# Attention scores on two halves of the contraction rows, with a running maximum from PSUM

## The chip, the cores and the metric

The kernel runs on one core of a Trainium2 chip. The metric is the device time in microseconds; three runs of the kernel before gave 732.77, 735.24 and 737.40 us. The times of single instructions come from one profiled execution.

## The reference, cut to what matters

```python
def _attn_ref(q, k, v):                       # 2 batches, 8 heads, 1152 rows, 64 columns, float32
    q_pool = q.reshape(B, H, S // 2, 2, D).mean(axis=3)
    scores = (1.0 / np.sqrt(D)) * np.matmul(q_pool, k.transpose(0, 1, 3, 2))
    scores = scores - np.max(scores, axis=-1, keepdims=True)
    attn = np.exp(scores)
    attn = attn / (np.sum(attn, axis=-1, keepdims=True) + 1e-09)
    return np.matmul(attn, v)
...
x = attention output as 1152 tokens x 512
x = softplus(x @ w_in1) @ w_out1              # 512 -> 2048 -> 512
h = x @ w_in2                                 # 512 -> 2048
g = (a0 + a1*h + a2*h*h + a3*h*h*h) / (1 + |b0|*|h| + |b1|*h*h + 1e-6)
out = g @ w_out2                              # 2048 -> 512
```

The queries are averaged in pairs, so a head has 576 queries and 1152 keys. The weights of the two MLPs come as 64-bit floats.

## The kernel before

Every product is wanted at nearly float32 accuracy. The kernel gets it by splitting an operand into a high half (rounded to the matmul's fast format, float32r) and a low half (the rest) and by multiplying hi x hi, hi x lo and lo x hi.

**Attention** goes through 16 heads, each in two units of 288 queries. A head loads q and k (lines 362 and 365), adds pairs of queries (line 373) and makes high and low halves in SBUF: `qs` holds hi, lo and once more the whole, `ks` holds hi and lo side by side. Line 285 is the subtraction that gives a low half, lines 270, 272 and 274 are copies on ACT, DVE and POOL; for all heads but the first this splitting is POOL's. PE transposes three blocks at a time (`trans_k`, line 395; `trans_q`, line 407), and ACT or DVE copies the result to SBUF. So a transposed key block fills all 128 contraction rows, 64 with its high half and 64 with its low half, and one block of scores takes two matmuls over 128 rows (line 487).

A unit computes scores for nine key blocks, two at a time into a tile `sc` of two PSUM banks, of which there are two in turn. ACT copies each to `st` in SBUF (line 497). When all nine are there, DVE takes the maximum over the nine blocks in one reduction (line 443); PE transposes it (450), DVE reduces it over partitions (454), PE spreads it back to all partitions (460), DVE subtracts it in two pieces of 1152 and 1440 columns (506), ACT takes the exponential (512). The first four blocks are multiplied with v in float32, the other five as high and low halves (543).

**The MLPs** go through 2 layers x 2 halves of the hidden width x 3 chunks of 384 tokens, and in each through 8 blocks of 128 hidden columns: twelve matmuls for h (663), an activation on ACT, POOL and DVE (687 to 702, or 715 to 731), and nine or twelve matmuls into four accumulating banks (745). Each weight piece is converted by three DVE instructions (621, 624, 627) and then split into halves, the high one by ACT, the low one by POOL, or by DVE for the hidden blocks in `VLO`.

**What sets the order.** Nothing is issued as it is written: each step is recorded with an engine, a duration, what it reads and writes, and a due time, and `Plan.order` places all of them by list scheduling with the durations of `act_t`, `dve_t`, `pool_t`, `pe_t`. The due times come from the tables `OFF` and `OFF2`. Each engine then works strictly in the order found. Buffers are slots in two SBUF arenas and the eight PSUM banks; `lay` sets them side by side, and a slot of the MLPs on bytes of attention is free only after attention's last tile there.

## Time and profile before

| | |
|---|---|
| median of 3 runs | 735.24 us (732.77 to 737.40) |
| span of the profiled execution | 731.1 us |
| PE, weight loads, DVE, ACT, POOL busy | 91%, 83%, 90%, 77%, 78% |
| instructions | 11574 |
| the reduction of line 443 | 32 times, 155.7 us |
| scores, line 487 | 576 matmuls of 128 rows x 288 columns |

A busy share counts the time in which an engine has at least one instruction in flight. Instructions of one engine overlap a little at their ends, so the distance between two starts is less than the duration printed. In a timeline a row is one instruction or a run of the same kind (x8), with the start of the first and the time to the end of the last. `a<-b` reads "into a from b"; `arena` and `arena_r` are the two SBUF arenas, `banks` is PSUM.

### The profile page before, as it was taken

How to read it: one execution, taken by the hardware profiler on the slowest of the kernel's cores; microseconds unless marked ns; L12 is line 12 of the kernel's file. 1: busy time of each engine (PE TensorE's matmuls, PEld its weight loads, DVE VectorE, ACT ScalarE, POOL GpSimd, SP SyncE). 2: the span in 40 equal slices, each digit the busy share in tenths (PEclk: the TensorE clock that was granted, in tenths of full speed). 3: DMA queues.
4: the chain of work that ended last, by engine and by line, in shares of the span. 5: the costliest groups of instructions: out<-in, count | busy, mean ns of one | idle time of the engine just before them, and what ended most of it. 6: DMA issues, size and time to landing. Idle time of an engine off the chain costs nothing.

```text
span 731.1 us, 11574 instructions
## 1 busy us (share of the span) xinstructions
PE 667.6 (91%) x4036; PEld 607.8 (83%) x4036; DVE 658.7 (90%) x694; ACT 566.5 (77%) x1029; POOL 567.9 (78%) x549
## 2 busy tenths in 40 slices
PE   7877888888888888869999999999999999999997
PEld 6766777777777777748999999999999899998996
DVE  4899999999999999999898898988697888879896
ACT  5777778887777777678788887878978888987764
POOL 5557686868677765669878898788999989998764
PEclk9899999999999999999999999999999999999999
DMA  8222212222121121425377678777012011211001
GB/s 210 65 59 58 58 48 52 50 57 51 48 52 51 23 83 25 139 69 160 115 234 227 203 230 260 242 256 252 30 55 61 15 30 43 59 30 44 0 31 57
DMA packets 66665, 70.02 MB, mean 96 GB/s; under 512 B 24496, under 2 KB 50096, under 8 KB 66608
## 3 DMA queue, kind: packets, MB, share of 16 engines
q1 hardware_dynamic: 66608, 69.30, 32.7%
q8 instruction: 31, 0.51, 0.3%
q14 instruction: 26, 0.21, 0.1%
HBM read 58.46 MB, written 10.78 MB: 95 GB/s over the span
## 4 chain that ended last, share of the span: by engine, by line
PE 58%; DVE 29%; issue 6%; ACT 3%; POOL 2%; DMA 1%; SPq 1%; DVEq 0%; POOLq 0%; ACTq 0%
PE banks L745 25%; PE banks L663 25%; DVE arena L443 17%; DVE arena L506 6%; PE banks L543 4%; PE banks L487 3%; DVE arena_r L272 2%; PE banks L407 1%; DVE arena L454 1%; PE banks L450 1%; POOL arena_r L285 1%; ACT arena L713 1%; DVE banks L727 1%; DMA arena<-rr 1%; DMA par<-in_moe_b_dram 1%
## 5 line engine op out<-in xcount | busy, mean ns | idle before, releaser
L285 POOL TENSOR_TENSOR arena_r<-arena,arena_r 128x512 fp32r<-128x512 f32 (+4 forms) x134 | 227.6, 1708 | 37.9 <-ACT arena_r L270 35.6
L745 PE MATMUL banks<-arena_r 128*128 128x384 f32 (+1 forms) x1008 | 212.6, 360 | 0.3 <-POOL arena_r L285 0.2
L663 PE MATMUL banks<-xh,arena_r 128*128 128x384 f32 x768 | 210.1, 337 | 2.6 <-DVE arena_r L285 1.8
L745 PEld LDWEIGHTS banks<-arena_r 128*128 128x128 f32 x1008 | 182.0, 188 | 15.8 <-POOL arena_r L285 0.6
L443 DVE TENSOR_REDUCE arena<-arena 128x288 f32<-128x2592 f32 x32 | 155.7, 4867 | 4.2 <-ACT arena L270 4.2
L270 ACT COPY arena<-banks 128x576 f32<-128x576 f32 (+4 forms) x213 | 115.3, 562 | 45.3 <-PE banks L543 26.4
L663 PEld LDWEIGHTS banks<-xh,arena_r 128*128 128x128 f32 x768 | 139.6, 188 | 6.0 <-DVE arena_r L285 3.2
L663 PE MATMUL banks<-xl,arena_r 128*128 128x384 f32 x384 | 128.8, 335 | 0.0
L727 DVE RECIPROCAL banks<-arena 128x384 f32<-128x384 f32 x48 | 122.6, 2555 | 6.5 <-ACT arena L713 5.0
L285 POOL TENSOR_TENSOR arena<-arena 128x384 f32<-128x384 f32 x96 | 98.8, 1030 | 26.2 <-ACT arena L697 19.5
L487 PE MATMUL banks<-arena_r 128*128 128x288 f32 x576 | 110.1, 315 | 0.2 <-ACT arena L270 0.2
L270 ACT CAST arena_r<-banks 128x384 fp32r<-128x384 f32 (+2 forms) x168 | 79.0, 472 | 39.2 <-PE banks L407 21.0
L506 DVE TENSOR_TENSOR arena<-arena,banks 128x1152 f32<-128x1152 f32 x64 | 93.4, 1501 | 0.6 <-PE banks L460 0.6
L487 PEld LDWEIGHTS banks<-arena_r 128*128 128x128 f32 x576 | 86.1, 191 | 6.5 <-ACT arena L270 1.6
L543 PE MATMUL banks<-arena_r 128*65 128x288 f32 (+1 forms) x480 | 87.8, 304 | 0.8 <-ACT arena_r L270 0.8
L512 ACT ACTIVATE arena<-arena 128x1152 f32<-128x1152 f32 x64 | 82.7, 1295 | 5.8 <-DVE arena L506 5.8
L270 ACT CAST arena_r<-arena 128x512 fp32r<-128x512 f32 (+2 forms) x90 | 79.9, 905 | 5.4 <-DVE arena L373 2.8
L543 PE MATMUL banks<-arena 128*65 128x288 f32 x256 | 80.0, 421 | 3.8 <-ACT arena L512 2.8
L285 DVE TENSOR_TENSOR arena_r<-banks,arena_r 128x384 fp32r<-128x384 f32 (+1 forms) x104 | 58.1, 560 | 27.6 <-ACT arena_r L270 27.2
L663 PEld LDWEIGHTS banks<-xl,arena_r 128*128 128x128 f32 x384 | 72.1, 188 | 1.1
L274 POOL TENSOR_SCALAR arena_r<-arena 96x384 fp32r<-96x384 f32 (+2 forms) x62 | 32.9, 539 | 46.2 <-PE banks L395 21.8
L719 POOL TENSOR_TENSOR arena<-arena 128x384 f32<-128x384 f32 x48 | 48.9, 1019 | 18.5 <-ACT arena L713 16.8
(54 smaller groups left out, 949.8 us busy)
## 6 DMA issues: line engine op xcount, KB each, us to landing
arena<-in_moe_w_in_dram SPq DMA_DIRECT2D x32, 512.0 KB, 4.4
arena<-in_moe_w_out_dram SPq DMA_DIRECT2D x32, 512.0 KB, 3.9
sp<-arena SPq DMA_DIRECT2D x32, 256.0 KB, 2.9
arena<-sp SPq DMA_DIRECT2D x32, 256.0 KB, 2.7
arena<-in_q_dram SPq DMA_DIRECT2D x16, 288.0 KB, 4.5
arena<-in_k_dram SPq DMA_DIRECT2D x16, 288.0 KB, 4.1
arena<-in_v_dram SPq DMA_DIRECT2D x16, 288.0 KB, 4.0
arena<-rr SPq DMA_DIRECT2D x16, 144.0 KB, 4.0
```

Source lines behind the costliest of these rows:

```text
L270: nc.scalar.copy(o, i)
L274: nc.gpsimd.tensor_scalar(out=o, in0=i, scalar1=1.0, scalar2=0.0, op0=ALU.mult, op1=ALU.add)
L285: e.tensor_tensor(out=o, in0=a, in1=b, op=ALU.subtract)
L443: P.op("V", dve_t(KC * HW), lambda: nc.vector.tensor_reduce(out=mx(), in_=st().rearrange("p c q -> p q c"), axis=AX.X, op=ALU.max), r=[(st ...
L487: nc.tensor.matmul(out=ps()[:, c, 0:HW], lhsT=kT()[:, c0 + c, :], rhs=qT[i]()[:, hf * HW:(hf + 1) * HW], start=(i == 0), stop=(i == 1),)
L506: nc.vector.tensor_tensor(out=s, in0=s, in1=mB()[:, None, :].to_broadcast([128, n, HW]), op=ALU.subtract)
L512: nc.scalar.activation(out=s, in_=s, func=AF.Exp, scale=escale)
L543: nc.tensor.matmul(out=o, lhsT=w, rhs=x, start=first, stop=last, skip_group_check=True)
L663: nc.tensor.matmul(out=hp(), lhsT=w()[:, kk * 128:(kk + 1) * 128], rhs=x[:, kk, :], start=(kk == 0 and n == 0), stop=(kk == KD - 1 and n = ...
L719: P.op("G", pool_t(CW), lambda: nc.gpsimd.tensor_tensor(out=Q(), in0=t(), in1=ah(), op=ALU.add), r=[t, ah], w=[Q], at=a("2q"))
L727: P.op("V", (69 + 6.25 * CW) / 1e3, lambda: nc.vector.reciprocal(out=h(), in_=Q()), r=[Q], w=[h], at=a("2r"))
L745: nc.tensor.matmul(out=o()[:, 0:w_], lhsT=lt, rhs=rh, start=(f == 0 and n == 0), stop=(f == FG - 1 and n == 2),)
```

## The change

Four things are changed, and the order of the whole program is found anew.

1. Queries and keys are no longer split in SBUF. PE transposes them in float32, two key blocks in one transpose (so the keys of block 2j lie on rows 0 to 63 and those of block 2j+1 on rows 64 to 127), and each pair of queries stands twice, on both halves of the rows. Out of PSUM, ACT writes the high half and DVE subtracts the low half. There are now four tensors `k1`, `k2`, `q1`, `q2`.
2. The scores of two key blocks come from six matmuls of 64 rows, three on each half of the rows, in turn, each half into its own bank; the lone ninth block takes three.
3. The maximum is kept as it goes: the scores of blocks 2 and 3 are compared with those of blocks 0 and 1 in SBUF, and those of each later pair with the running maximum `mp`, always read from the score tile in PSUM; the last block joins the two halves.
4. `VLO` is empty: POOL subtracts the low halves of all weights. The constants of the second MLP are loaded after the fifth head's reciprocals.

```diff
-VLO = (3, 4, 5, 6)
+VLO = ()
-M0 = 464.257
-WAIT = 0.2
-SLACK = 0.05
+M0 = 295.089
+QKT = 0.46
+WAIT = 0.093
+SLACK = 0.005
 def pe_t(n, cols):
-    return n * max(cols / 2.4 + 3, 107.0) / 1e3
+    return n * (cols / 2.4 + 13.5) / 1e3
...
-    r1 = lay(0, arena_r, 0, LR, ("qs", 1, 4608), ("ks", 1, 4608), *kq, *kq)
+    r1 = lay(0, arena_r, 0, LR, *kq, *kq)
...
+            def pool_q():
+                x = [qr()[:, :, r, :][:, :, None, :].to_broadcast([96, NQQ, 2, D]) for r in range(2)]
+                (nc.vector if first else nc.gpsimd).tensor_tensor(out=qm(), in0=x[0], in1=x[1], op=ALU.add)
...
+            def halves(t, n, np_, src, dst, keys, at):
+
+                hi, lo = dst
+                P.op("A", act_t(n), lambda: cp("A", hi(), src()), r=[t], w=[keys[0]], at=at)
+                P.op("V", dve_t(n), lambda: sub("V", lo(), src(), hi()), r=[t, keys[0]], w=[keys[1]], at=at)
...
+                js = [(0, 1, 2), (3, 4)][g]
...
+                for lo, hi, np_ in ((js[0], js[-1] + 1, 128),) if g == 0 else ((3, 4, 128), (4, 5, 64)):
...
-            mx = P.buf("mx", [128, HW], F32)
-            P.op("V", dve_t(KC * HW), lambda: nc.vector.tensor_reduce(
-                out=mx(), in_=st().rearrange("p c q -> p q c"), axis=AX.X, op=ALU.max),
-                r=[(st, c) for c in range(KC)], w=[mx], at=t0 + OFF['mx'] * T)
...
-                for c in range(n):
-                    for i in range(2):
+                for x, (a, y) in enumerate(((0, 0), (0, 1), (1, 0))):
+                    for i in range(n):
                         nc.tensor.matmul(
-                            out=ps()[:, c, 0:HW],
-                            lhsT=kT()[:, c0 + c, :],
-                            rhs=qT[i]()[:, hf * HW:(hf + 1) * HW],
-                            start=(i == 0),
-                            stop=(i == 1),
+                            out=ps()[:, i, 0:HW],
+                            lhsT=kT[a]()[64 * i:64 * i + 64, j, :],
+                            rhs=qT[y]()[64 * i:64 * i + 64, hf * HW:(hf + 1) * HW],
+                            start=(x == 0),
+                            stop=(x == 2),
                         )
...
+            def top(o, x, y, m, r, w):
+                P.op("V", dve_t(m * HW), lambda: nc.vector.tensor_tensor(out=o(), in0=x(), in1=y(), op=ALU.max),
+                     r=r, w=w, at=t0 + (OFF['mx'] + 0.15 * j) * T)
+
+            if j == 1:
+                top(mp, lambda: ps()[:, :, 0:HW], lambda: st()[:, 0:2, :], 2, [ps, (st, 0), (st, 1)], [mp])
+            elif n == 2 and j:
+                top(mp, lambda: ps()[:, :, 0:HW], mp, 2, [ps], [mp])
+            elif n == 1:
+                half = lambda: ps()[:, 1, 0:HW]
+                top(half, lambda: ps()[:, 0, 0:HW], lambda: mp()[:, 0, :], 1, [ps, mp], [(ps, 1)])
+                top(mx, half, lambda: mp()[:, 1, :], 1, [(ps, 1), mp], [mx])
...
-        ), w=["par"], at=M0, xfer=0.11)
+        ), r=[("rr", 4)], w=["par"], at=M0, xfer=0.11)
```

All entries of `OFF` and `OFF2` are replaced too, and the order that comes of it is best seen in the program's own rows. First DVE in the middle of attention, before, from one partition reduction of the maximum on to the next: the maximum over all keys (L443), the two subtractions (L506), the normalisation (L559, L560), an eviction of transposed keys (L272).

```order
L454 TENSOR_REDUCE arena<-banks 96x3
L443 TENSOR_REDUCE arena<-arena 128x288
L506 TENSOR_TENSOR arena<-arena,banks 128x1152
L506 TENSOR_TENSOR arena<-arena,banks 128x1440
L559 TENSOR_SCALAR arena<-arena 64x9
L560 RECIPROCAL arena<-arena 64x9
L272 COPY arena_r<-banks 128x384
```

The same place now, where L496 is the partition reduction, L543 the running maximum, L332 the low halves of a head's keys, L561 the subtraction.

```order
L496 TENSOR_REDUCE arena<-banks 96x3
L543 TENSOR_TENSOR arena<-banks,arena 128x576
L332 TENSOR_TENSOR arena_r<-banks,arena_r 128x384
L543 TENSOR_TENSOR arena<-banks,arena 128x576
L561 TENSOR_TENSOR arena<-arena,banks 128x1152
L543 TENSOR_TENSOR arena<-banks,arena 128x576
L332 TENSOR_TENSOR arena_r<-banks,arena_r 128x128
L543 TENSOR_TENSOR banks<-banks,arena 128x288
L332 TENSOR_TENSOR arena_r<-banks,arena_r 64x128
L543 TENSOR_TENSOR arena<-banks,arena 128x288
L561 TENSOR_TENSOR arena<-arena,banks 128x1440
```

The one long maximum has become five short ones, and other work stands between any two of them that hang on each other.

PE in the middle of attention, before: scores (L487) between pieces of PV (L543) and the transposes of queries (L407) and of the maximum (L450).

```order
L450 MATMUL banks<-ident,arena 96x128 x3
L543 MATMUL banks<-arena_r 65x288 x2
L407 MATMUL banks<-identr,arena_r 128x96 x3
L543 MATMUL banks<-arena_r 65x288 x2
L487 MATMUL banks<-arena_r 128x288 x8
L407 MATMUL banks<-identr,arena_r 128x96 x3
```

And now, with L529 the scores, L441 the transposes of keys, L492 and L502 those of the maximum, L598 PV:

```order
L441 MATMUL banks<-ident,arena 128x128 x3
L492 MATMUL banks<-ident,arena 96x128 x3
L598 MATMUL banks<-arena_r 65x288 x2
L529 MATMUL banks<-arena_r 128x288 x12
L598 MATMUL banks<-arena 65x288 x3
L502 MATMUL banks<-ident,arena 128x96 x3
L598 MATMUL banks<-arena 65x288
L529 MATMUL banks<-arena_r 128x288 x6
```

Scores now come in groups of six (the size printed is that of the output), and the transposes read float32 data (`ident,arena`) straight.

POOL where attention ends, before, from its last low half of probabilities (128x1440) on; L694 and the 128x384 subtractions belong to the MLP's activation, 128x512 is the low half of a weight.

```order
L285 TENSOR_TENSOR arena_r<-arena,arena_r 128x1440
L694 TENSOR_SCALAR arena<-arena 128x384
L285 TENSOR_TENSOR arena<-arena 128x384
L285 TENSOR_TENSOR arena_r<-arena,arena_r 128x512
L285 TENSOR_TENSOR arena<-arena 128x384
```

And now:

```order
L332 TENSOR_TENSOR arena_r<-arena,arena_r 128x1440
L332 TENSOR_TENSOR arena_r<-arena,arena_r 128x512
L749 TENSOR_SCALAR arena<-arena 128x384
L332 TENSOR_TENSOR arena<-arena 128x384
L332 TENSOR_TENSOR arena_r<-arena,arena_r 128x512
L332 TENSOR_TENSOR arena<-arena 128x384
L332 TENSOR_TENSOR arena_r<-arena,arena_r 128x512
```

A low half of a weight now stands beside nearly every step of the activation, where before it stood beside every second or third.

## Rows read from the trace of the kernel before

**Rows 1.** The page's first part: busy us, share of the span, instructions.

```profile
PE 667.6 (91%) x4036; PEld 607.8 (83%) x4036; DVE 658.7 (90%) x694; ACT 566.5 (77%) x1029; POOL 567.9 (78%) x549
```

**Rows 2.** Stretches: from:to, length, busy us by engine, granted clock, DMA, GB/s.

```profile
132.30:151.10 18.80, 15.84 (x117) 13.73 (x116) 18.52 (x16) 14.77 (x23) 15.42 (x15) 1.00 0.24 57
...
540.00:560.00 20.00, 20.00 (x101) 17.96 (x100) 17.85 (x17) 18.27 (x38) 19.51 (x19) 1.00 0.14 41
```

**Rows 3.** DVE's timeline over one head: start us, us, instruction.

```profile
169.85 4.87 DVE L443 TENSOR_REDUCE arena<-arena 128x288 f32<-128x2592 f32 x1
174.65 2.90 DVE L506 TENSOR_TENSOR arena<-arena,banks 128x1152 f32<-128x1152 f32 x2
177.47 0.15 DVE L559 TENSOR_SCALAR arena<-arena 64x9 f32<-64x9 f32 x1
...
177.84 0.56 DVE L272 CAST arena_r<-banks 128x384 fp32r<-128x384 f32 x1
178.31 0.54 DVE L454 TENSOR_REDUCE arena<-banks 96x3 f32<-96x384 f32 x1
178.78 4.89 DVE L443 TENSOR_REDUCE arena<-arena 128x288 f32<-128x2592 f32 x1
183.59 2.90 DVE L506 TENSOR_TENSOR arena<-arena,banks 128x1152 f32<-128x1152 f32 x2
186.41 0.45 DVE L272 CAST arena_r<-banks 128x288 fp32r<-128x288 f32 x1
186.78 0.73 DVE L573 TENSOR_TENSOR arena<-arena 64x576 f32<-64x576 f32 x1
187.77 0.46 DVE L272 CAST arena_r<-banks 128x288 fp32r<-128x288 f32 x1 [0.26 <-PE banks L407]
...
188.61 4.90 DVE L443 TENSOR_REDUCE arena<-arena 128x288 f32<-128x2592 f32 x1
```

**Rows 4.** Groups by line and shape: count, busy us, mean ns, idle before.

```profile
L285 DVE TENSOR_TENSOR arena_r<-banks,arena_r 128x384 fp32r<-128x384 f32 x96 | 52.8, 550 | 25.8 <-ACT arena_r L270 25.5
...
L285 DVE TENSOR_TENSOR arena_r<-banks,arena_r 128x512 fp32r<-128x512 f32 x8 | 5.4, 680 | 1.8 <-ACT arena_r L270 1.8
...
L487 PE MATMUL banks<-arena_r 128*128 128x288 f32 x576 | 110.1, 315 | 0.2 <-ACT arena L270 0.2
...
L270 ACT CAST arena_r<-banks 128x288 fp32r<-128x288 f32 x32 | 12.9, 402 | 21.3 <-PE banks L407 21.0
...
L270 ACT CAST arena_r<-banks 128x384 fp32r<-128x384 f32 x128 | 61.7, 483 | 17.3 <-DVE banks L699 9.5 <-DVE banks L728 6.3 <-PE banks L395 0.9
...
L285 POOL TENSOR_TENSOR arena_r<-arena,arena_r 128x512 fp32r<-128x512 f32 x56 | 72.8, 1305 | 1.9 <-ACT arena_r L270 1.9
```

**Rows 5.** PE's timeline over the same head.

```profile
183.72 0.53 PE L450 MATMUL banks<-ident,arena 128*96 128x128 f32 x3 [1.51 <-DVE arena L443]
184.01 0.51 PE L543 MATMUL banks<-arena_r 128*65 128x288 f32 x2
...
184.84 1.23 PE L487 MATMUL banks<-arena_r 128*128 128x288 f32 x8
185.91 0.36 PE L407 MATMUL banks<-identr,arena_r 96*128 96x96 f32 x3
186.11 0.68 PE L543 MATMUL banks<-arena 128*65 128x288 f32 x2
...
187.57 1.17 PE L543 MATMUL banks<-arena 128*65 128x288 f32 x4
188.36 0.58 PE L407 MATMUL banks<-identr,arena_r 96*128 96x96 f32 x3
```

**Rows 6.** DVE's timeline: the last pair of subtractions of a maximum.

```profile
321.57 2.90 DVE L506 TENSOR_TENSOR arena<-arena,banks 128x1152 f32<-128x1152 f32 x2
```

**Rows 7.** Stretches at the start of the MLPs, columns as in Rows 2.

```profile
321.50:340.00 18.50, 16.16 (x92) 14.19 (x91) 16.94 (x26) 13.94 (x26) 15.75 (x15) 1.00 0.49 146
340.00:360.00 20.00, 19.73 (x111) 18.83 (x110) 18.08 (x31) 16.34 (x35) 17.59 (x21) 1.00 0.45 139
```

## What the change will do to the time: the prediction

> **What bounds the kernel now.** I read the busy shares first, then the same shares in stretches of the span, then one head of attention on VectorE's timeline. The page gives PE 91% and DVE 90% [rows 1], an average over two stages with different limits. The stretches part them. While one head of attention passes (18.8 us), DVE is busy 18.52 us, PE 15.84, ACT 14.77 and POOL 15.42 [rows 2]; in the second stage, as from 540 to 560 us, PE is busy for 20.00 us out of 20.00 and DVE for 17.85. So DVE sets the pace up to its last subtraction of a maximum, which ends at 324.4 us [rows 6], and PE sets it from there to the end.
>
> Inside a head DVE's instructions follow each other without a gap: from 169.85 to 188.61 us stand two maxima over all keys (start to next start 4.80 us each), two pairs of subtractions (2.82 each), the small reductions, three evictions of transposes and the normalisation, 18.76 us in all, of which about 0.25 is idle [rows 3]. The maximum alone is half of that. What matters for the sum is the distance from start to start, which is 0.08 to 0.09 us less than the duration printed (the eviction at 177.84 prints 0.56, and the next instruction starts 0.47 later) [rows 3].
>
> **The change, step by step, for one head (two units) in the steady stretch.**
>
> *DVE.* Removed: two maxima, 2 x 4.80 = 9.60, and three evictions, 0.47 for 384 columns and 2 x 0.37 for 288 columns, 1.21 in all [rows 3]. Added per unit: three maxima of 576 columns and two of 288 that read the score tile in PSUM. The trace has no such instruction; the nearest are subtractions of two tensors with one in PSUM, 0.550 us at 384 columns and 0.680 at 512 [rows 4], less 0.085 each: 0.465 and 0.595, or 1.016 ns a column. That gives 0.66 for 576, 0.367 for 288, and 3 x 0.66 + 2 x 0.367 = 2.71 a unit, 5.43 a head. Added per head: the low halves of keys and queries are now subtracted from PSUM by DVE, one of 384 columns, two of 128 (0.205 each) and two of 288: 0.465 + 0.41 + 0.73 = 1.61. So 18.76 - 0.25 - 9.60 - 1.21 + 5.43 + 1.61 = **14.7 us a head**. If the maximum cost per column what the old reduction does (4.80 / 2592 = 1.85 ns) it would be 3 x 1.07 + 2 x 0.53 = 4.27 a unit and 17.9 a head; I take the subtraction's rate, since form and operands are its own and the reduction walks the keys with a stride.
>
> *PE.* Eight score matmuls of 288 columns pass in 1.07 us, 0.134 each; three transposes of 96 rows in 0.20; four fp32 passes in 0.79; three fp32 transposes in 0.29 [rows 5]. Before, a unit is 18 x 0.134 = 2.41 for the scores and 8 x 0.198 + 15 x 0.134 + 0.29 + 0.20 = 4.08 for the rest; with 21 transposes of queries and keys (1.40) a head is 14.4, where the window shows 15.84 busy [rows 2] because the end of each burst counts. After, there are 11 fp32 transposes a head (11 x 0.097 = 1.06), and two key blocks take six matmuls of 64 rows in place of four of 128. They stand on two halves of the rows and write two banks. Nothing in the trace is of this kind. Lower bound: the halves run at once, three turns, 0.40 us for the six; upper bound without any other loss: they queue, six turns, 0.80. I take 0.50: three turns as rows and banks are separate, and 0.1 for what the change of shape costs. The lone last block is 0.40. Then a head is 2 x (4 x 0.50 + 0.40 + 4.08) + 1.06 = 14.0 (13.2 at the lower bound, 16.5 at the upper).
>
> The Trainium skill speaks on both sides here. TensorEngine Tiling, Key Properties, says that a change of tiling mode drains the engine; each score group would enter and leave such a mode, and by the price that the first rival below takes for that, the sum would be its 710. TensorE: Matmul & The Clock Gate, Part 3 (Measured speedup vs the span model), gives four concurrent row tiles 3.07 times the speed; by that the six would take hardly more than three turns, an estimate of 0.42, and the time below would not move. No row here can show either.
>
> *ACT.* One eviction of 384 columns becomes three (384, 128, 128) in place of two of 384; by 0.402 for 288 and 0.483 for 384 [rows 4] the two short ones together come to about 0.5, so nothing changes: 14.8 busy a head [rows 2]. *POOL* loses five of its six operations on queries and keys, all but an addition that doubles in width; it had room (15.4 of 18.8) and has more. The query's and key's low halves no longer wait for it.
>
> *The new wait.* A score tile now goes back to PE only when DVE has taken its maximum too, with two tiles in turn. Behind a waiting score group PE holds the PV matmuls and the transposes of the other unit, and DVE waits for those. At the tightest place of the new order two maxima on the same slot have 0.37 + 0.66 + 0.37 = 1.4 us of other DVE work between them, against 0.50 us on PE plus handovers (PE's transposes start 0.05 us after the reduction's end, 183.72 against 183.67 [rows 3, 5]). That hides it as long as PE is not in the middle of a run of PV matmuls.
>
> *The pace.* DVE 14.7, ACT 14.8 busy, PE 14.0 to 15: three engines within a few per cent, where before one stood alone and lost 1% [rows 2]. That a bound engine can stay full beside near-full ones, the second stage shows at 540 us (PE 20.00 of 20.00, POOL 19.51, ACT 18.27) [rows 2]. I take **15.3 us a head**, 4% over DVE's sum.
>
> *The hand-over to the MLPs.* The order has three weight conversions ahead of DVE's last subtraction, before it was five; each is three instructions of about 0.69. And all low halves of weights go to POOL: behind its last 128x1440 subtraction 14 of them stand in the first eight tiles, four before, at 1.305 us [rows 4], 13 us more work on POOL, which was idle 2.75 + 2.41 us between 321.5 and 360 [rows 7]. DVE gets rid of eight such subtractions (5 us) and takes two conversions more (4 us). So 0 to 8 us are lost here; PE works ahead on up to three tiles, I take 4. From there on PE's matmuls are the same in number and size and PE is full [rows 2], so the order that the new numbers make changes nothing as long as weights come in time. The load of the four constants for the second MLP moves from the start behind a head of attention, and nothing near waits for it: nothing.
>
> **The sum.** Before: 324.4 us = 16 x 18.76 = 300.2, and 24.2 for start, last units and five conversions. After: 16 x 15.3 = 244.8, and 24.2 - 4 = 20.2: the last subtraction ends at 265. Behind it before: 731.1 - 324.4 = 406.7 [rows 6]; after 410.7. Span 675.7. The median of the runs shown is 4.1 us above the profiled span (735.24 against 731.1), so **680 us**.
>
> **The rivals.**
> - *The rows are split, but not for free (18%).* Either the halves queue (0.80, PE 16.5 a head), or they overlap and each change of shape lets the array run empty: a matmul lasts 0.315 us and starts every 0.134 [rows 4, 5], so 0.18 a change, 0.36 a group, 0.76 with the lone block alike: 2 x (5 x 0.76 + 4.08) + 1.06 = 16.8. For it: 20 changes a head; against it: nothing is known of the array's cost of a change. PE then sets 17.2 a head: 680 + 16 x 1.9 = **710**. That is what TensorEngine Tiling's rule would do at this price.
> - *Both, and the kernel is slower (6%).* Queueing and running empty: 0.80 + 0.36 = 1.16 a group, 2 x (4 x 1.16 + 0.76 + 4.08) + 1.06 = 20.0, at 2% over it 20.4 a head: **762**. It is slower than before from 0.95 us a group on (18.7 a head).
> - *The two readers of a score tile take turns (4%).* ACT's copy and DVE's maximum read the same bank; if DVE stood still for each whole copy (0.65 for 576 columns by the two rows for ACT, 0.40 for 288 [rows 4]), 2 x 2.35 = 4.7 a head come on top, 19.4: **745** at worst, no change if half of it overlaps. Against it: DVE has other work in between, and a wait can be moved.
> - *Everything fits (6%).* DVE at 14.7 and no loss at the hand-over: 680 - 10 - 4 = **666**, or some us below.
>
> **How the numbers follow.** My forecast, three engines near the pace of 14.7 to 16.1 a head and 0 to 8 us at the hand-over, gets 66%: 664 to 697. With the first rival up to 718 and the best case down to 662 the range leaves out some 18%. A per cent (7 us) is about what can be told from no change, as the three runs differ by 4.6 us. Faster by more than that are the forecast, the first and the last case, less a little for their ends: 0.88; within it 0.04; slower 0.08.
>
> **What would show it.** Right: the start-to-start time of a head near 15.3 us with DVE above 93% busy; six score matmuls within 0.4 to 0.55 us; 576-column maxima of some 0.75 us; DVE's last subtraction near 265 us; PE full from about 310 us. Wrong: six score matmuls in 0.76 us or more, with PE the busiest engine of a head and DVE waiting for score tiles; maxima of 1.1 us; a first chunk of the MLPs in which PE waits for POOL's 128x512 subtractions for more than 8 us; or holes in PE's second stage, which I count as none.

## The result, and the profile after

The changed kernel takes 711.48 us (median of four runs, 711.2 to 714.15), the kernel before 736.24 beside it: a ratio of 0.9685 (95% interval 0.9658 to 0.9712), 25 us faster. The forecast was 680 us, 55 us faster. The time lies in the range given (662 to 718 us), and almost on the first rival (710 us); the likeliest case was not the one that came.

The page's first part of the kernel after, to be laid beside [rows 1]:

```profile
span 709.4 us, 11978 instructions
...
PE 689.3 (97%) x4164; PEld 583.8 (82%) x4164; DVE 609.4 (86%) x844; ACT 568.9 (80%) x1043; POOL 527.3 (74%) x481
```

Two stretches of attention, columns as in [rows 2] (length, then busy us of PE, PEld, DVE, ACT, POOL, granted clock, DMA share, GB/s):

```profile
149.00:165.00 16.00, 16.00 (x122) 11.59 (x121) 15.09 (x23) 14.16 (x24) 11.28 (x8) 1.00 0.23 62
...
180.00:196.00 16.00, 16.00 (x118) 11.26 (x118) 15.03 (x25) 14.54 (x22) 11.08 (x9) 1.00 0.23 66
```

PE is full from the first of these microseconds to the last; DVE, the bound before [rows 2], is at 94%. The small reduction of a unit comes back after two units:

```profile
155.16 0.54 DVE L496 TENSOR_REDUCE arena<-banks 96x3 f32<-96x384 f32 x1
...
171.96 0.54 DVE L496 TENSOR_REDUCE arena<-banks 96x3 f32<-96x384 f32 x1
```

That is **16.8 us a head**, where 18.8 was before and 15.3 was forecast. What PE does in such a head is read from the chain of work (start us, us from one step's end to the next one's, engine, line, count), which here is PE alone. L529 are the score matmuls, L598 the PV matmuls, L455 and L441 the transposes of queries and keys, L492 and L502 those of the maximum:

```profile
157.64 0.60 PE banks L529 x6
158.24 0.63 PE banks L598 x2
158.87 0.59 PE banks L529 x3
159.47 0.40 PE banks L455 x3
...
163.25 0.99 PE banks L529 x12
164.24 1.60 PE banks L598 x6
165.84 0.28 PE banks L502 x3
166.12 0.49 PE banks L598 x2
166.60 0.60 PE banks L529 x6
...
167.82 0.59 PE banks L529 x3
168.42 1.86 PE banks L598 x13
```

Twelve score matmuls, two groups in a row, take 0.99 us, a single group of six 0.60: the second six cost 0.39, three turns of 0.134 [rows 5]. So the two halves of the rows do run at once, and 0.2 us are paid on the way into the shape of 64 rows. The way out is paid by what stands behind: the same two fp32 PV matmuls take 0.49 behind a transpose and 0.63 behind a score group, 0.14 more. The lone last block, three matmuls, pays both as well. The two together, 0.34 us, fall due some eight times a head.

The last subtraction of a maximum ends at 287.7 us (forecast 265, before 324.4 [rows 6]); behind it come 421.7 us (forecast 410.7, before 406.7). In DVE's timeline its start and length are:

```profile
286.06 1.65 DVE L561 TENSOR_TENSOR arena<-arena,banks 128x1440 f32<-128x1440 f32 x1
```

### The profile page after: what moved, and what is told of

It reads as the page before. It is cut to its first block, busy times and chain, and to the rows that moved or that the text cites. A ratio compares the mean times of both kernels' runs of the same rounds, so it can differ in the third digit from the quotient of the medians.

```text
span 709.4 us, 11978 instructions
## 1 busy us (share of the span) xinstructions
PE 689.3 (97%) x4164; PEld 583.8 (82%) x4164; DVE 609.4 (86%) x844; ACT 568.9 (80%) x1043; POOL 527.3 (74%) x481
## 4 chain that ended last, share of the span: by engine, by line
PE 73%; DVE 10%; POOL 6%; DMA 4%; issue 3%; ACT 3%; SPq 0%; POOLq 0%; DVEq 0%; ACTq 0%
PE banks L718 21%; PE banks L800 20%; PE banks L598 15%; PE banks L529 11%; POOL arena_r L332 2%; DVE arena L543 2%; DMA arena<-rr 2%; PE banks L492 1%; PE banks L455 1%; PE banks L441 1%; ACT arena L317 1%; DVE banks L782 1%; POOL arena L332 1%; DMA arena<-in_moe_w_in_dram 1%; POOL arena L778 1%
## 5 line engine op out<-in xcount | busy, mean ns | idle before, releaser
L332 POOL TENSOR_TENSOR arena_r<-arena,arena_r 128x512 fp32r<-128x512 f32 (+2 forms) x112 | 201.5, 1804 | 91.8 <-ACT arena_r L317 84.4
L800 PEld LDWEIGHTS banks<-arena_r 128*128 128x128 f32 x1008 | 181.0, 188 | 24.6 <-ACT arena_r L317 6.2
L317 ACT COPY arena<-banks 128x576 f32<-128x576 f32 (+4 forms) x213 | 114.8, 558 | 29.9 <-PE banks L529 15.9
L332 POOL TENSOR_TENSOR arena<-arena 128x384 f32<-128x384 f32 x96 | 98.1, 1024 | 18.2 <-ACT arena L752 13.6
L529 PE MATMUL banks<-arena_r 64*128 64x288 f32 x864 | 102.8, 330 | 4.5 <-DVE arena L543 1.8
L529 PEld LDWEIGHTS banks<-arena_r 64*128 64x128 f32 x864 | 70.9, 192 | 43.5 <-issue 13.4
L332 DVE TENSOR_TENSOR arena_r<-banks,arena_r 128x384 fp32r<-128x384 f32 (+3 forms) x176 | 84.1, 481 | 26.3 <-ACT arena_r L317 26.1
L317 ACT CAST arena_r<-banks 128x384 fp32r<-128x384 f32 (+3 forms) x176 | 73.3, 427 | 38.5 <-DVE banks L754 15.1
L543 DVE TENSOR_TENSOR arena<-banks,arena 128x576 f32<-128x576 f32 (+1 forms) x128 | 85.7, 670 | 15.3 <-ACT arena L317 10.8
L561 DVE TENSOR_TENSOR arena<-arena,banks 128x1152 f32<-128x1152 f32 x64 | 95.4, 1490 | 0.3 <-PE banks L502 0.3
L317 ACT CAST arena_r<-arena 128x512 fp32r<-128x512 f32 (+1 forms) x96 | 83.9, 887 | 8.5 <-DVE arena L682 6.3
L598 PE MATMUL banks<-arena_r 128*65 128x288 f32 (+1 forms) x480 | 81.2, 305 | 0.0
L598 PE MATMUL banks<-arena 128*65 128x288 f32 x256 | 78.6, 417 | 1.4 <-ACT arena L317 1.4
L598 PEld LDWEIGHTS banks<-arena_r 128*65 128x65 f32 (+1 forms) x480 | 59.9, 136 | 6.6 <-issue 5.7
```

The costliest lines, as they stand in the source:

```text
L317: nc.scalar.copy(o, i)
L332: e.tensor_tensor(out=o, in0=a, in1=b, op=ALU.subtract)
L529: nc.tensor.matmul(out=ps()[:, i, 0:HW], lhsT=kT[a]()[64 * i:64 * i + 64, j, :], rhs=qT[y]()[64 * i:64 * i + 64, hf * HW:(hf + 1) * HW], s ...
L543: P.op("V", dve_t(m * HW), lambda: nc.vector.tensor_tensor(out=o(), in0=x(), in1=y(), op=ALU.max), r=r, w=w, at=t0 + (OFF['mx'] + 0.15 * j ...
L561: nc.vector.tensor_tensor(out=s, in0=s, in1=mB()[:, None, :].to_broadcast([128, n, HW]), op=ALU.subtract)
L598: nc.tensor.matmul(out=o, lhsT=w, rhs=x, start=first, stop=last, skip_group_check=True)
```

## The experiments

**What a change of shape costs.** Three kernels with the order of the kernel after, in each of which only the operands of the score matmuls are other ones.

*e1, the lone block on all rows.* The last block's scores are made with the keys of another pair.

```
-  lhsT=kT[a]()[64 * i:64 * i + 64, j, :],
+  lhsT=kT[a]()[64 * i:64 * i + 64, j, :] if n == 2 else kT[a]()[:, 3, :],
   (rhs likewise: qT[y]()[:, ...] where n == 1)
```

> The changed kernel, except that the three score matmuls of the lone ninth key block run over all 128 rows (it multiplies two other blocks' rows, so these scores are not the reference's). Number, width and order of all instructions stay. Theory 1 (each excursion of PE to 64-row matmuls and back costs it about 0.35 us; PE is the bound in attention): this group falls from 0.59 us to 0.40 and what follows it loses its late start, 0.34 us a unit, 32 units, 11 us: 700 us, period of a head 16.1 us instead of 16.8. Theory 2 (no cost of a change; the 0.59 is a wait for a score tile that the trace calls busy): group and time stay, 711 us.

Measured: 707.35 us, ratio 0.9618 (0.9592 to 0.9644). In the chain the lone block's three matmuls and the thirteen PV matmuls behind them now read:

```profile
165.96 0.40 PE banks L529 x3
166.35 1.71 PE banks L598 x13
```

0.19 and 0.15 us less than at 167.82 and 168.42 above: the price of one excursion is 0.34 us, in and out. But two of them a head are 0.68, and the head became only 0.35 us shorter (16.45). Its stretch says why:

```profile
150.00:200.00 50.00, 49.31 (x376) 36.81 (x375) 48.63 (x74) 45.24 (x72) 31.87 (x20) 1.00 0.23 66
```

DVE is at 97%. Close behind PE stands DVE, with 16.0 us a head and not the 14.7 of the forecast; the experiments e12 to e14 take that up.

*e2, both halves on the same rows* (the second half's scores are made from the first half's keys):

```
-  lhsT=kT[a]()[64 * i:64 * i + 64, j, :],
+  lhsT=kT[a]()[0:64, j, :],                  (rhs likewise 0:64)
```

> The changed kernel, except that the six score matmuls of a pair of blocks all use rows 0 to 63 (so the second block gets the first one's scores). Shape, number and order stay. If the two halves of the rows do run at once in the changed kernel, six now take six turns of 0.134 us: 0.40 us more for each of four groups a unit, 1.6 a unit, 51 us in all: 762 us, head 20.0 us. If they queue already and the changes of shape cost nothing, nothing moves: 711 us.

Measured: 760.67 us, ratio 1.0343 (1.0305 to 1.038). A single six takes 0.98 us and a second six behind it 0.79, six turns:

```profile
149.86 1.77 PE banks L529 x12
...
153.97 0.98 PE banks L529 x6
```

So it is the separate rows that make the halves overlap, and the 0.19 us of entry is paid here too: it belongs to the shape, not to the overlap. This is also the second rival of the prediction run for itself (762 us): without the overlap the change would have been a loss.

*e3, every score matmul on 128 rows*, six and three as before (each block then sums over both blocks of its pair):

```
-  lhsT=kT[a]()[64 * i:64 * i + 64, j, :],
+  lhsT=kT[a]()[:, min(j, 3), :],             (rhs likewise, all rows)
```

> The changed kernel with all score matmuls over 128 rows, still six for a pair and three for the lone block (two blocks' scores are summed, so they are not the reference's). No change of shape is left, and no overlap of halves. Theory 1: a group is 0.80 us and costs nothing on either side, 4 x 0.80 + 0.40 = 3.6 us a unit against 2.78 us for the groups and some 0.6 behind them now: head 16.8 to 17.3 us, 711 to 719 us. If changes of shape cost nothing, the unit grows by 0.8 us: head 18.4, 737 us.

Measured: 715.3 us, ratio 0.9719 (0.9684 to 0.9754). A group costs 0.80, the lone block 0.40, and what stands behind has its low price again:

```profile
151.41 0.22 PE banks L441 x2
...
151.90 0.40 PE banks L529 x3
152.29 1.70 PE banks L598 x13
154.00 0.80 PE banks L529 x6
```

0.80 without a change of shape against 0.60 and 0.15 with one. A head takes 17.2 us in place of 16.8; in the whole the split is worth some 4 us out of the 25 against the same matmuls on all rows, which the intervals of the two ratios do not part.

**What the running maximum carries.** *e4* leaves out two of the three maxima of 576 columns in each unit, so the shift of the exponent is the maximum over fewer keys. *e5* puts the old reduction back.

```
e4: -  top(mp, lambda: ps()[:, :, 0:HW], mp, 2, [ps], [mp])
    +  P.op("V", dve_t(2 * HW), lambda: None, r=[ps], w=[mp], at=...)
e5: -  the calls of top()
    +  P.op("V", dve_t(KC * HW), lambda: nc.vector.tensor_reduce(
    +      out=mx(), in_=st().rearrange("p c q -> p q c"), axis=AX.X, op=ALU.max), ...)
```

> The changed kernel without the running maximum's second and third step (the maximum is taken over five of nine blocks; the softmax is shifted by less). It takes 2 x 0.66 us a unit from DVE, 2.6 us a head, and frees two score tiles earlier; PE's instructions and all orders stay. Theory 1 (PE is the bound): head stays at 16.6 to 16.8 us, 708 to 711 us. Theory 3 (DVE, or the score tile that waits for DVE, sets the pace and PE's busy share hides it): head falls by 1.5 us or more, 687 us or less.

> The kernel after, with its running maximum taken out and the old maximum over all nine key blocks (one reduction of 128x2592 from SBUF) put back. What the running maximum alone is worth beside the other two parts. In the kernel after PE sets 16.8 us a head and DVE is busy some 15.8. The five maxima of a unit cost 3 x 0.66 + 2 x 0.37 = 2.7 us from start to start, the reduction 4.8: DVE's sum becomes 15.8 + 2 x 2.1 = 20.0 us a head. If DVE then sets the pace: 711 + 16 x (20.0 - 16.8) = 762 us, slower than the kernel before, and DVE above 97% busy in a head with PE waiting. If the slowed multiply of the normalisation gives back its 2 x 0.75 once POOL and DVE no longer meet: 18.5 us a head, 738. Below 725 would say that DVE was not near the bound, and that the maximum is not what pays for the change.

Measured: e4 707.85 us (0.9624, 0.9575 to 0.9673). DVE falls to 39.7 of 50 us, PE stays at 50.00 of 50, and a head takes 16.8 us. DVE's work was not the bound. e5 797.51 us (1.0835, 1.0774 to 1.0896), 35 us beyond the 762 expected. There the planner puts the rest in another order too, since the reduction needs all nine blocks: PE has holes of its own.

```profile
100.00:150.00 50.00, 39.79 (x261) 27.03 (x259) 43.38 (x38) 33.23 (x54) 22.39 (x14) 0.90 0.16 42
```

So without the running maximum the other parts make a kernel slower than before, in the order that comes of the same table. What they would do with a table chosen for them, no run shows.

*e10* is the opposite: the kernel before with the running maximum, and without the split rows and the split in PSUM. Its layout has no room for low halves of weights on DVE, so POOL subtracts all of them as in the kernel after, and its table is a new one.

> The kernel before with the running maximum alone: queries and keys are cut on POOL, ACT and DVE in SBUF and transposed as before, the scores are 128-row matmuls as before, and all low halves of weights are on POOL, since the layout that makes room for the running maximum has no more slots; the table that orders the work is chosen anew. DVE: 18.5 - 9.6 + 5.4 = 14.3 us a head (15.9 if the multiplication meets POOL each time); PE 2 x (18 x 0.134 + 4.54) + 21 x 0.067 = 15.3; POOL 15.4, as in the kernel before. If the running maximum alone carries the gain of the kernel after: 15.6 to 16.2 us a head, 690 to 702 us. If POOL's queue, which the kernel after relieves, sets the pace: above 16.8 us a head, 710 us or more, with POOL above 95% busy in a head.

Measured: 718.73 us, ratio 0.9764 (0.9717 to 0.9811), beside the 690 to 702 expected. In the steady stretch a head takes 16.6 us, which is the pace of the whole change:

```profile
100.00:150.00 50.00, 48.38 (x349) 41.60 (x349) 44.81 (x69) 44.74 (x68) 42.50 (x37) 1.00 0.26 64
```

What it loses to the kernel after lies ahead of that stretch: its fourth small reduction comes at 58.9 us, there at 43.5, and its last subtraction ends at 295.4 us, with 423.0 behind it. In attention's pace the row split and the split in PSUM bring nothing beyond the running maximum, in the orders that were run.

**The hand-over to the MLPs.** Two tries to get the 15 us back: *e6a* returns eight low halves of weights to DVE, *e6b* takes the MLPs' table of the kernel before, which has 13 weight conversions ahead of the last subtraction instead of 3.

```
e6a: -VLO = ()            e6b: -OFF2, M0 of after
     +VLO = (3, 4, 5, 6)       +OFF2, M0 of before
```

> The kernel after, with the low halves of the weights of first-layer tiles 3 to 6 back on DVE, as in the kernel before (eight subtractions of 128x512 from POOL to DVE). The time behind DVE's last subtraction of a maximum is 421.8 us in the kernel after and 406.7 before. If POOL's queue of low halves (1.3 us each) is what came late there: 8 x 1.3 = 10 us come off POOL's queue, the time behind falls to 410 to 414, and the whole to 699 to 704 us. If DVE's conversions came late instead, DVE has 8 x 0.6 = 5 us more to do ahead of the same matmuls: 711 to 717.

> The kernel after, with the table of numbers that orders the MLPs (and their due time) as in the kernel before; attention's table stays that of the kernel after. In this order 13 weight conversions, of three DVE instructions each, stand ahead of DVE's last subtraction of a maximum, in place of 3. If the late conversions make the 15 us behind the last subtraction: 10 conversions x 2.05 = 20 us of DVE's work move into attention, where DVE has some 1.0 us a head to spare while PE sets the pace; the time behind falls from 422 to 403 to 408 us, attention gains 0 to 5: 695 to 702 us. If POOL's low halves are it, or weights that wait for a tile: 708 to 715. If the conversions hold up attention (they share a PSUM bank with the transposes): above 720.

Measured: e6a 714.32 us (0.972, 0.9687 to 0.9753), 425.1 us behind the last subtraction: with less in POOL's queue of low halves nothing comes sooner. e6b 753.56 us (1.0263, 1.0213 to 1.0314), 421.6 us behind. Its hand-over itself is mended: 36 first-layer matmuls stand ahead of the last subtraction as in the kernel before (12 in the kernel after), and PE is idle 3.3 us in the 80 us behind it (7.3 in the kernel after). But a new hole of 5 us stands 210 us later in its MLPs, and attention is 47 us longer. It is not the conversions between DVE's instructions that cost this: PE has holes in every stretch (46.24 of 50 us from 100 to 150 us), and in that one DVE has no conversion at all. The planner places both stages together, so attention's instructions stand in another order too; in it some multiplications of the normalisation take 3 us and more (3.07 at 120.43). So early conversions go with a better hand-over; what they alone would cost attention, this run does not show.

**The multiplication that became slow.** DVE's sum was 14.7 us by the forecast and 16.0 in e1. Most of the difference, 1.1 to 1.2 us, is one instruction, the multiplication of the normalisation (L573 before, L628 after), 0.73 us in [rows 3]. Timelines of DVE and of POOL in the kernel after:

```profile
163.30 1.83 DVE L628 TENSOR_TENSOR arena<-arena 64x576 f32<-64x576 f32 x1
```

```profile
162.70 1.82 POOL L418 TENSOR_TENSOR arena<-arena 96x768 f32<-96x768 f32 x1
```

POOL's addition ends at 164.52, the multiplication 0.61 us later. In other heads it is the same: at 112.03 it takes 1.83 us and ends 0.61 behind the addition, at 129.81 it takes 1.42 and ends 0.61 behind. In the kernel before the multiplications stand in POOL's gaps (median 0.75). That the operand has just come by DMA is not the reason: at 299.29 us DVE stands 0.55 us for that DMA, and the multiplication right behind it takes 0.75.

*e7* moves the multiplication to POOL, and the planner then finds another order for all engines. *e12* leaves it on DVE and puts it two places later, all else in the old order.

```
e7:  -P.op("V", dve_t(SQ), lambda: nc.vector.tensor_tensor(
     +P.op("G", pool_t(SQ), lambda: nc.gpsimd.tensor_tensor(
e12: +  for nm in [z for z in seq if z.seq in P.norm]:   # behind P.order
     +      ... seq.insert(seq.index(to) + 1, nm)        # to: two DVE rows later
```

> The kernel after, with the multiplication of the normalisation (64x576, both inputs in SBUF) on POOL in place of DVE. In the kernel after it takes DVE 0.75 us where POOL is idle and 1.8 us where POOL runs. DVE's sum falls from 15.8 to some 13.5 to 14 us a head. If PE alone sets the pace: 16.8 us a head as before, 708 to 713 us. If DVE's late answers are part of the 16.8 us, PE shows gaps that close: 695 to 705. On POOL the multiplication should take about 1.0 to 1.5 us, whatever DVE does.

> The kernel after, with every multiplication of the normalisation two places later in DVE's order, behind the small reduction and a running maximum that follow it; every other engine's order is the same, row by row. In the kernel after each multiplication stands over POOL's addition of 96x768 and ends 0.6 us behind it (1.8 us instead of 0.75). If the two take turns at SBUF: the multiplication takes 0.75 to 0.85 us, DVE's sum falls from 15.8 to some 14.9 us a head, and as PE is full the time stays: 708 to 712. If the multiplication is slow for another reason (its operand that a DMA has just written), it stays at 1.4 us and more. If DVE's lateness is part of the 16.8 us: 700 to 707.

Measured: e7 735.05 us (0.9996, 0.9976 to 1.0016), all of the gain gone. The multiplication takes its wait along: it needs a DMA, and between 30 and 285 us POOL now stands for 31.3 us in all in front of it (eight times, 7.9 us at most), with the low halves of the exponentials behind it in its queue:

```profile
POOL arena L628 <- DMA arena<-rr: 31.3, 8, 7.9
```

How much of the loss is this wait and how much the new order, the run does not part.

e12 710.46 us (0.9654, 0.9633 to 0.9675), as expected with PE full. The instruction, now behind the addition's end, takes

```profile
164.72 0.74 DVE L629 TENSOR_TENSOR arena<-arena 64x576 f32<-64x576 f32 x1
```

(POOL's addition ran from 162.18 to 164.00), and DVE falls from 94% to 90%, 44.95 of 50 us. So the two instructions take turns. The Trainium skill has this in SBUF — State Buffer, section "SBUF: two separate sides": a VectorE instruction with two SBUF inputs and a GpSimd instruction that reads SBUF share a port pair, and whichever starts first has it until it ends. The trace agrees: the addition starts first, and the multiplication ends 0.61 us behind it, close to the 0.74 that it takes alone.

**Taking both away.** *e13* makes the ninth block whole on 128 rows (loaded twice, high half above low half, two matmuls in place of three), in the same order; *e14* adds e12's edit.

```
+  nc.sync.dma_start(out=kr()[:, KC, :], in_=kd[:, KC - 1, :])        # block 8 again
+  P.op("A", ..., lambda: cp("A", d(), src()), ...)                   # all 128 rows: high
+  P.op("V", ..., lambda: sub("V", d()[64:128], src()[64:128], d()[64:128]), ...)
+  for y in range(2 if n == 1 else 0):
+      nc.tensor.matmul(out=ps()[:, 0, 0:HW], lhsT=kT[0]()[:, j, :], rhs=qT[y]()[:, ...], ...)
```

> The kernel after, with the ninth key block's scores made whole on 128 rows: the block is loaded twice side by side, one transpose puts it on both halves of the rows, ACT copies all of them and DVE subtracts on rows 64 to 127, so that the high half lies above the low one; two matmuls of 128 rows (0.27 us) replace three of 64 rows (0.59 and 0.15 behind them). Order of all engines as in the kernel after. PE falls from 16.8 to 15.9 us a head, DVE stays at 15.8 to 16.0 with the slowed multiplication. In the kernel with the lone block's three matmuls on 128 rows DVE was the next bound at 16.45 us a head. If that holds here: 704 to 708. If the two engines' waits were of PE's making: 697 to 702.

> Both edits: the ninth block in two matmuls of 128 rows, and the multiplication two places later. PE 15.9 us a head, DVE 14.9, ACT 14.8. If the largest sum sets the pace once DVE has room: 15.9 to 16.2 us a head, 711 less 16 x (0.6 to 0.9): 697 to 702 us. If three engines near each other keep the 16.4 to 16.6 us of the kernels with full rows (16.6 us with sums of 15.3 and 15.2): 704 to 708, as with the ninth block's edit alone.

Measured: e13 708.36 us (0.9631, 0.9608 to 0.9655), e14 **704.39 us** (0.9583, 0.9549 to 0.9617). The stretch from 150 to 200 us, first of e13, then of e14:

```profile
150.00:200.00 50.00, 48.91 (x367) 35.78 (x366) 48.73 (x73) 44.71 (x72) 31.75 (x20) 1.00 0.24 65
```

```profile
150.00:200.00 50.00, 49.94 (x379) 37.26 (x378) 47.28 (x78) 45.98 (x73) 33.92 (x21) 1.00 0.28 77
```

In e13 DVE is at 97% and a head takes 16.6 us; in e14 PE is full again and a head takes 16.0 us, by PE's own sum 15.9. So it was the multiplication that stood behind PE as the next bound, not mutual waits over the score tiles. The pace is that of the first expectation, the time that of the second: e14's eleventh small reduction comes at 104.65 us, 1.2 us later than in the kernel after, so the shorter heads count only from there on. e14 leaves nothing out and is faster than both kernels.

*e9* goes on in that direction: no half rows at all, with a new table. *e11* is e1 (its lone block as there) with a table chosen anew by the measured prices.

```
e9:  -  kT = [P.buf("k1", ...), P.buf("k2", ...)]     # high, low: two blocks on two halves
     +  kT = P.buf("kT", [128, KC, 128], F32R)        # one block: high above low
     +  two matmuls of 128 rows a block; the normalisation's multiplication on POOL
e11: -P.op("P", QKT, mm, ...
     +P.op("P", QKT if n == 2 else 0.41, mm, ...      # QKT = 0.75; OFF, OFF2, M0 chosen anew
```

> A version in which no score matmul uses half of the rows, and which still splits into high and low halves in PSUM. The keys are loaded twice side by side, so that one transpose of 128 columns puts the same key block on rows 0 to 63 and 64 to 127; ACT copies all rows and DVE subtracts on rows 64 to 127, which gives the high half above the low half. The queries are there twice already. Two matmuls of 128 rows a block then give (kh + kl)(qh + ql), eight for every four blocks where the kernel after has twelve on half rows. The multiplication of the normalisation goes to POOL, the running maximum stays, and the table that orders the work is chosen anew for these instructions. PE by the measured prices: 2 x (18 x 0.134 + 4.54) + 15 transposes at 0.11 = 15.5 us a head, in place of 16.8; DVE 14.0 + 0.5 for one more low half = 14.6; ACT about 15.1. If the price of changing the array's shape is what the kernel after lost: 15.6 to 16.0 us a head, 695 us from that alone, and as 13 weight conversions stand ahead of DVE's last subtraction in this order (3 in the kernel after), 0 to 15 less behind it: 680 to 697. If something else holds the head at 16.8 us: 705 to 712.

> The kernel with the lone block on 128 rows (16.45 us a head, 707 us), with the table that orders the work chosen anew with the measured prices of a score group (0.75 with what it costs the matmuls behind it, 0.41 for the lone block) in place of 0.46 for both, and 1.4 us for the multiplication of the normalisation. Nothing else is changed. 11 weight conversions stand ahead of DVE's last subtraction, 3 before. If the order was only wrong in what it took for the prices: attention keeps 16.4 us a head, the 15 us behind the last subtraction shrink to 0 to 8, and the time is 692 to 700 us. If the conversions cost attention what they save behind it: 703 to 710.

Measured: e9 718.02 us (0.9756, 0.9717 to 0.9795), e11 724.8 us (0.9838, 0.9787 to 0.989), both far from what was expected. In e9 no engine is full:

```profile
150.00:200.00 50.00, 46.77 (x310) 37.33 (x309) 45.68 (x70) 45.88 (x68) 39.82 (x27) 1.00 0.33 78
```

The new orders put 13 and 11 weight conversions ahead of the last subtraction, as e6b did. Attention is longer (last subtraction at 301.3 and 306.4 us, against 287.7 in the kernel after and 283.5 in e1), and the 415.0 and 417.4 us behind it are less than in the kernel after. As attention's own table is another one too, it is not shown that the conversions are what attention pays for. Whether full rows in a better order would reach their sum of 15.5 us a head stays open: it was not tried in the order of the kernel after, as the transposes of keys are others.

## Why the prediction was right and wrong

**DVE: right in its parts, wrong in its sum.** The maxima of 576 columns print 0.69 to 0.76 us (forecast 0.75), those of 288 0.44 to 0.47, and the low halves come out as taken from [rows 4]. The third rival, readers of a score tile taking turns, did not come: a maximum keeps its 0.74 beside a copy of ACT's.

```profile
165.53 0.74 DVE L543 TENSOR_TENSOR arena<-banks,arena 128x576 f32<-128x576 f32 x1
...
165.73 0.63 ACT L317 COPY arena<-banks 128x576 f32<-128x576 f32 x1
```

What failed is a price carried over as fixed: the multiplication went from 0.75 to 1.8 us since the new order puts it beside POOL's addition. The sum was 15.8 to 16.0, and without that 15.0 to 15.1 (e12: 44.95 of 50 us, 16.77 a head), where 14.7 was forecast. As PE was full, this failure cost no time in the kernel after (e12); it showed once e1 and e13 gave PE room.

**PE: the step that failed.** The term is "I take 0.50: three turns as rows and banks are separate, and 0.1 for what the change of shape costs. The lone last block is 0.40." The three turns were right (e2, and 0.39 for a second six). The change of shape is 0.19 in and 0.15 out: 0.75 for a single group, 0.74 for the lone block. One head of the chain, from 154.79 to 171.59 us, against the forecast's 14.0:

- score matmuls 5.55 us in all, 4.8 forecast: 0.75 more;
- eight exits of 0.145: 1.16 more;
- sixteen fp32 passes of 0.245 (0.49 for two), taken as 0.198: 0.75 more;
- transposes of the maximum 0.33 and 0.25 to 0.28 a unit, in place of 0.29 and 0.20: 0.2 more.

14.0 and 2.86 is 16.86; measured 16.8. The 0.198 was read in [rows 5] from the start of one row of the timeline to the start of the next, 0.79 us for four passes. From end to end two such passes took 0.49 in the kernel before as well:

```profile
187.05 0.49 PE banks L543 x2
```

So 0.75 us of the gap between 14.4 and 15.84, which the prediction put down to the ends of bursts, was this.

The first rival had the mechanism and the price of a change (0.18), from the difference between a matmul's duration and its turn; the forecast set that price aside with the argument that nothing in the trace was of this kind. That the rival's head comes to 16.8 as well is in part luck: it counts 20 changes, 3.6 us, where eight entries and eight exits made 2.7, since some groups stand back to back, and the passes and transposes made up for the rest. Its 710 us is luck in part too: it took 17.2 us a head and lost 4 at the hand-over, where 16.8 and 15 were measured. What PE does in the 0.34 us the trace does not show. The Trainium skill's rule (TensorEngine Tiling, Key Properties) is that a change of tiling mode drains the engine; the trace agrees that the change has a price, here 0.34 us in and out. Its rule in the same list, that tiles work in parallel, holds as well, 0.39 us for six. Both hold at once, where the prediction weighed one against the other.

**The pace.** 15.3 was forecast and 16.8 measured: 16 x 1.5 = 24 us of the span's miss of 33.7; the hand-over makes 11 more. The forecast's 15.3 stood on DVE's sum, and PE's, taken as 14.0 to 15, was the larger one. That a full engine stays full beside near-full ones held (PE 16.00 of 16.00).

**The hand-over: 15 us, not 4.** The step that failed is "PE works ahead on up to three tiles". From 150 us to the last subtraction PE had these first-layer matmuls behind it in the kernel after:

```profile
L718 PE MATMUL banks<-xh,arena_r 128*128 128x384 f32 x8 | 2.2, 335 | 0.0
...
L718 PE MATMUL banks<-xl,arena_r 128*128 128x384 f32 x4 | 1.3, 334 | 0.0
```

And these in the kernel before:

```profile
L663 PE MATMUL banks<-xh,arena_r 128*128 128x384 f32 x24 | 7.1, 348 | 0.7 <-POOL arena_r L285 0.7
L663 PE MATMUL banks<-xl,arena_r 128*128 128x384 f32 x12 | 4.0, 336 | 0.0
```

12 in place of 36. While DVE set the pace PE worked ahead into the MLPs; with PE full, in this order, it does so less, and 24 matmuls (twelve pass in 2.1 us) are 4.2 us more behind the last subtraction. 42 PV matmuls stand there instead of 27, twelve of them fp32 instead of eight: 2.5 us. And once PE stands for longer: the stretch has 5.3 us of idle PE, and behind it the granted clock falls from full speed (2.4 GHz) to a mean of 0.77 of it, between its two levels (1.2 and 2.4 GHz):

```profile
307.60:317.60 10.00, 4.73 (x24) 4.15 (x24) 8.30 (x13) 5.29 (x12) 9.10 (x12) 0.89 0.67 208
317.60:327.60 10.00, 9.90 (x44) 9.60 (x45) 8.95 (x15) 6.13 (x14) 7.95 (x8) 0.77 0.65 195
```

Summed over the stretches of ten microseconds up to the end, PE is idle 11.6 us (7.3 before) and loses 2.8 us to the clock (0.4 before). 4.2 + 2.5 + 4.3 + 2.4 is 13.4 of the 15 us. The chain that ends the wait runs back to a DMA that the last multiplication of the normalisation needs. DVE stands 1.38 us for it, with the conversions (L676 to L682) behind the multiplication in its queue, and PE waits for the high half of an activation (ACT L317) that comes after them:

```profile
306.97 4.49 DMA arena<-rr
...
311.48 0.77 DVE arena L628
...
312.27 0.70 DVE arena L682
...
317.17 0.49 ACT arena_r L317
```

e6b, with ten more conversions early, has no such hole there, and e6a, with less work on POOL, has. This points at the late conversions, of which the forecast counted two (4 us) and set them against the eight subtractions that leave DVE; what they cost by themselves, and what that DMA costs, no run shows.

**What else was forecast.** The start cost what was taken for it within 1.4 us, and the reload of the constants cost nothing. The chances had the sign right; the 18% for the first rival was too little for a price that two rows pointed to.

## What to carry to other kernels

Splitting the contraction rows pays only where several split groups stand back to back: count the entries and exits of the shape as instructions with a price (0.34 us here), and compare with the same work on full rows. Here the kernel before needs four matmuls of 128 rows for two key blocks, 0.54 us, and a split group 0.40 and its share of the 0.34, so by these prices (an estimate) it takes three groups in a row to win on PE. When the bound moves from one engine to another, ask what the old bound's slack was paying for elsewhere: here PE's idle time had carried matmuls of the next stage. And before a duration is carried over from the old trace, look at what will run beside it on the engine that shares its way to memory; moving an instruction two places gave its duration back, while on another engine it took its wait along.

## What the runs showed of the hardware

A 64x576 multiplication of two SBUF operands on DVE that starts beside a running POOL addition of 96x768 ends 0.61 us behind it: 0.74 us alone, up to 1.85 beside it. Going into matmuls of 64 rows costs PE 0.19 us whether or not the halves overlap (e2, 0.98 for six on the same rows), and coming out 0.15; a second group in the same shape is free of both. An fp32 pass of 288 columns takes 0.245 us from end to end (0.49 for two), an fp32r matmul 0.134.
